# Banded attention and two feed-forward layers: six norms traced a part per step, and four conversion steps instead of five

## The chip, the cores and the metric

The kernel runs on one core of a Trainium2 chip. The core has five engines with a queue each that is worked off in order: TensorE (PE in the rows) for matmuls, VectorE (DVE), ScalarE (ACT), GpSimd (POOL) and SyncE (SP), which here only issues transfers (DMA). The metric is the device time of one execution in microseconds.

## The reference

Three stages follow each other, each on the result of the one before. The attention has 4 batches of 8 heads with 512 local and 32 global positions and a head width of 64. Local queries see the global keys and the local keys within 32 positions; global queries see all.

```python
    s_ll = np.where(mask, s_ll, -1000000000.0)
    s_l = np.concatenate([s_lg, s_ll], axis=-1)
    out_l = np.matmul(sm(s_l), np.concatenate([v_g, v_l], axis=2))
    ...
    rms = np.sqrt(np.mean(x * x, axis=-1, keepdims=True) + 1e-06)
    xn = x / rms * rms_g
    g = xn @ w_gate
    silu = g * (1.0 / (1.0 + np.exp(-g)))
    x = silu * (xn @ w_val) @ w_out
    ...
    h = x @ w_in
    g = P(h) / (Q(h) + 1e-06)
    return g @ w_out
```

The second stage (FFN1) has 2304 tokens, a width of 512 and a hidden width of 1536, the third (FFN2) a hidden width of 2048 and a rational function with P of third and Q of second degree. The weights arrive in 64-bit floating point.

## The kernel before

**Stages.** The loop over t from 0 to 35 (in the function that the program prints below) runs the attention, a pair of heads and half of the positions at a time: `att.step(t, between)` traces scores (`psS`), softmax (`p`, `pt`), products (`psO`, `on`) and the turned result (`psX`, copied to `x` at L420); `qt` at L338 are the turned queries of a step. For each pair of heads there is also a part for the global queries (`psG`, `pg`, `psGT`, `ptg`, `psOg`, `og`, `psGX`). Between these pieces `unit()` traces units of FFN1, 60 of them within the loop; FFN1 has three groups of weights by eight blocks of tokens, in the order 1, 0, 3, 2, 5, 4, 7, 6. A unit multiplies the split activations `xt` (L615, L616: a rounded part and its rest) by `w_g` and `w_v` (L625, L626, L629: `psg`, `psv`), applies the gate (L640 to L644: `a`, `ah`, `al`) and multiplies by `w_o` (L653 to L655: `psA`). After the loop comes the rest of FFN1, then FFN2.

**Norms.** Before the first unit of a block its tokens are normed. `norm_stages` is a generator with two `yield`s, so it has three parts: squares on ScalarE (L584, L585, L587, L589) and their sums on GpSimd (L586, L588, L590); then the sum over channels by a matmul `psN` (L593), L594 on VectorE and L595 on ScalarE; then L598 to L600 twice and the scaling L603 on VectorE. `norm_step()` runs the next part of the oldest norm. `split` runs whatever parts are left when a block's `xt` is made.

**Weights.** `Weights.stages` turns a 64-bit weight tile `raw` into two 32-bit ones, in four steps of a generator: L83 and L85 on ScalarE (L85 works in place on `raw`, so it needs the transfer of `raw` to have landed), L91, L92 and L95 on VectorE, L99 on VectorE, and L104 on ScalarE with the subtraction L105 on GpSimd. `wts.step` moves two such jobs on by one step and starts another when one is done. The transfers of `raw` (`raw_g`, `raw_v`, `raw_o`) are issued by SyncE at L66, in one queue with the loads of attention inputs at L216 (`vw`, `vn`, `gin`, `qin`, `kin`); a `vw` buffer is loaded, and then rounded off by small copies `vw<-vw`, once the `psO` that read it is done.

**What sets the order.** The code only traces instructions. A scheduler orders every engine's queue by priority, and by place in the trace at like priority. `att.step` is traced at an offset of 50 from t = 5, the norm parts at one of 200 (a higher one goes first), units and conversion steps at plain priority.

Of the kernel before, what the change touches and what calls it, by code (L numbers as in the profile page):

```python
# [788 lines left out]
def kernel(  # L789
# [20 lines left out]
    def load_consts():  # L810
        nc.sync.dma_start(out=gam, in_=rms_g.rearrange("(c p) -> p c", p=128))
        nc.sync.dma_start(out=av, in_=bass.AP(tensor=ca.tensor, offset=ca.offset, ap=[[0, 128], [1, 4]]))
        nc.sync.dma_start(out=bv, in_=bass.AP(tensor=cb.tensor, offset=cb.offset, ap=[[0, 128], [1, 2]]))
# [29 lines left out]
    def norm_step():  # L843
        if norms and next(norms[0], StopIteration) is StopIteration:
            norms.pop(0)

    def unit():
        done[0] += 1
        next(units, None)
# [24 lines left out]
    for t in range(LAST + 1):  # L874
        if t >= SECOND:
            target[0] = 6 + (IN_ATTN - 6) * (t + 1 - SECOND) / (LAST + 1 - SECOND)
        elif t >= START:
            target[0] = 6 * (t + 1 - START) / (SECOND - START)
        gate = [i.ins for i in (att.last_exp, att.last_ttr) if i]
        with tc.high_priority(offset=50) if t >= START else nullcontext():  # L880
            att.step(t, between)
        while done[0] < target[0] - 1:
            unit()
        if t == 2:
            load_consts()
        if t % 4 == 2 and t > 12:
            norms.append(ffn.norm(ORD[(t - 6) // 4]))
        elif t in (4, 8):
            norms.append(ffn.norm(ORD[t // 4 - 1]))
        with tc.high_priority(offset=200):  # L890
            for _ in range(3):
                norm_step()
        for _ in range(2 if t > 2 else 0):
            if loads:
                with tc.issue_after(att.last_dma.ins):
                    loads.pop(0)()
        with ExitStack() as late:
            for i in gate if t <= 8 else ():
                late.enter_context(tc.issue_after(i))
            for _ in range((0, 0, 0, 2, 5, 4, 4, 4)[t] if t < 8 else 2):  # L900
                wts.step(nc.gpsimd)
    while done[0] < IN_ATTN:
        unit()
# [94 lines left out]
```

## Time and profile before

| | us |
|---|---|
| median of 3 runs | 1048.28 (1047.91 to 1048.77) |
| profiled execution | 1043.17 |
| its span | 1041.4 |
| TensorE busy in it | 987.8 |
| VectorE busy | 779.1 |
| ScalarE busy | 633.0 |
| GpSimd busy | 189.2 |

The profile covers one execution; its span is the time from its first to its last instruction. All durations come from this one execution, whose time is 5.1 us under the median of the runs. Busy times of engines overlap. The granted clock of TensorE is a share of its full 2.4 GHz: at 0.50 it runs at 1.2 GHz.

### The profile page before, as it was taken

The page shows a single profiled execution, that of the slowest core. Times are in us where ns is not written, and L with a number is a line of the kernel's source. Part 1 is how long each engine was busy: PE and PEld are TensorE (multiplying, and loading weights), DVE is VectorE, ACT ScalarE, POOL GpSimd, SP SyncE. Part 2 cuts the span into 40 slices and gives each one's busy share as a digit, 9 for nine tenths or more (in the row PEclk, how much of TensorE's full clock was granted, in tenths as well). Part 3 has the DMA queues.
Part 4 walks back from the last instruction along what each step waited for, and adds up shares of the span by engine and source line. Part 5 has one row for each costly group of instructions (what it writes and reads, how often), then busy time and mean ns, then how long its engine had stood idle before and what let it go on. Part 6 is the DMA issues. An engine that isn't in the chain of part 4 may idle for free.

```text
span 1041.4 us, 23568 instructions
## 1 busy us (share of the span) xinstructions
PE 987.8 (95%) x9376; PEld 900.6 (86%) x9376; DVE 779.1 (75%) x1848; ACT 633.0 (61%) x1442; POOL 189.2 (18%) x220
## 2 busy tenths in 40 slices
PE   7578989999989999999999999999999999999997
PEld 5366877887879999999999999989899889899895
DVE  6586553655549899884896444898988989889897
ACT  4546554645457774553754323777777778777685
POOL 5333221202120000000000002321222222222222
PEclk8669999999999999999999999999999999999999
DMA  9733645353143421542501106200000000000000
GB/s 239 202 106 80 142 115 130 82 142 82 31 165 140 163 82 50 212 166 82 179 24 41 42 1 202 82 1 24 8 1 31 1 2 31 1 32 1 1 31 21
DMA packets 103311, 82.38 MB, mean 79 GB/s; under 512 B 63137, under 2 KB 90785, under 8 KB 103201
## 3 DMA queue, kind: packets, MB, share of 16 engines
q1 hardware_dynamic: 101472, 74.58, 24.2%
q0 software_dynamic: 1728, 6.29, 1.8%
q8 instruction: 74, 1.21, 0.5%
q14 instruction: 37, 0.30, 0.1%
HBM read 62.64 MB, written 10.75 MB: 70 GB/s over the span
## 4 chain that ended last, share of the span: by engine, by line
PE 80%; DVE 9%; DMA 5%; ACT 3%; SPq 1%; issue 1%; POOL 0%; ACTq 0%; POOLq 0%; DVEq 0%
PE psH L731 6%; PE psH L733 6%; PE psH L732 6%; PE psB L767 6%; PE psB L768 6%; PE psB L769 5%; PE psg L625 5%; PE psA L653 4%; PE psv L625 4%; PE psg L626 4%; PE psv L626 4%; PE psA L655 4%; PE psA L654 4%; PE psv L629 4%; PE psg L629 4%; PE psS L364 3%
## 5 line engine op out<-in xcount | busy, mean ns | idle before, releaser
L758 POOL TENSOR_TENSOR gl<-p,gh 128x384 fp32r<-128x384 f32 (+1 forms) x94 | 95.2, 1013 | 281.2 <-ACT gh L756 239.1
L731 PE MATMUL psH<-yt,w_h 128*128 128x384 f32 (+1 forms) x384 | 125.6, 328 | 0.5 <-DVE y L661 0.5
L732 PE MATMUL psH<-yt,w_h 128*128 128x384 f32 (+1 forms) x384 | 125.6, 327 | 0.0
L733 PE MATMUL psH<-yt,w_h 128*128 128x384 f32 (+1 forms) x384 | 123.5, 328 | 0.0
L625 PE MATMUL psg<-xt,w_g 128*128 128x288 f32 (+1 forms) x384 | 113.8, 299 | 7.7 <-ACT xt L615 7.6
L653 PE MATMUL psA<-ah,w_o 128*128 128x288 f32 (+1 forms) x384 | 112.8, 297 | 2.4 <-DVE y L661 1.1
L625 PE MATMUL psv<-xt,w_v 128*128 128x288 f32 (+1 forms) x384 | 111.1, 292 | 0.0
L626 PE MATMUL psv<-xt,w_v 128*128 128x288 f32 (+1 forms) x384 | 110.7, 290 | 0.0
L767 PE MATMUL psB<-w_p,gh 128*128 128x512 f32 x272 | 108.0, 397 | 2.9 <-ACT gh L756 2.9
L626 PE MATMUL psg<-xt,w_g 128*128 128x288 f32 (+1 forms) x384 | 110.3, 290 | 0.0
L654 PE MATMUL psA<-ah,w_o 128*128 128x288 f32 (+1 forms) x384 | 109.9, 290 | 0.0
L655 PE MATMUL psA<-al,w_o 128*128 128x288 f32 (+1 forms) x384 | 109.4, 290 | 0.0
L768 PE MATMUL psB<-w_p,gh 128*128 128x512 f32 x272 | 107.5, 395 | 0.0
L629 PE MATMUL psv<-xt,w_v 128*128 128x288 f32 (+1 forms) x384 | 103.4, 291 | 0.0
L629 PE MATMUL psg<-xt,w_g 128*128 128x288 f32 (+1 forms) x384 | 102.6, 289 | 0.0
L741 DVE SCALAR_TENSOR_TENSOR q<-q,bv,t 128x384 f32<-128x384 f32 (+1 forms) x96 | 67.6, 704 | 29.6 <-ACT q L739 29.4
L769 PE MATMUL psB<-w_p,gl 128*128 128x512 f32 x272 | 84.7, 395 | 0.0
L625 PEld LDWEIGHTS psg<-xt,w_g 128*128 128x128 f32 x384 | 72.7, 190 | 10.5 <-ACT xt L615 8.2
L751 ACT ACTIVATE r<-q,cq 128x384 f32<-128x384 f32 (+1 forms) x96 | 57.6, 600 | 36.7 <-DVE q L741 36.0
L653 PEld LDWEIGHTS psA<-ah,w_o 128*128 128x128 f32 x384 | 72.9, 190 | 4.4 <-DVE y L661 1.5
L731 PEld LDWEIGHTS psH<-yt,w_h 128*128 128x128 f32 x384 | 72.3, 188 | 3.9 <-DVE y L661 0.8
L732 PEld LDWEIGHTS psH<-yt,w_h 128*128 128x128 f32 x384 | 72.3, 188 | 3.7
(176 smaller groups left out, 2635.6 us busy)
## 6 DMA issues: line engine op xcount, KB each, us to landing
raw_h<-in_moe_w_in_dram SPq DMA_DIRECT2D x16, 512.0 KB, 3.7
raw_p<-in_moe_w_out_dram SPq DMA_DIRECT2D x16, 512.0 KB, 4.5
vw<-vw SPq DMA_DIRECT2D x56, 130.0 KB, 2.6
raw_g<-in_moe_w_gate_dram SPq DMA_DIRECT2D x12, 512.0 KB, 4.2
raw_v<-in_moe_w_val_dram SPq DMA_DIRECT2D x12, 512.0 KB, 5.2
raw_o<-in_moe_w_out_dram SPq DMA_DIRECT2D x12, 512.0 KB, 6.0
vw<-in_v_l_dram SPq DMA_DIRECT2D x62, 80.0 KB, 2.5
out_dram<-o SPq DMA_DIRECT2D x17, 256.0 KB, 2.0
```

The costliest lines, as they stand in the source:

```text
L625: nc.tensor.matmul(ps[j], part(j, 0, c), xt[c][:, 0], start=(c == 0), stop=False)
L626: nc.tensor.matmul(ps[j], part(j, 1, c), xt[c][:, 0], start=False, stop=False)
L629: nc.tensor.matmul(ps[j], part(j, 0, c), xt[c][:, 1], start=False, stop=(c == 3))
L653: nc.tensor.matmul(ps, wh, ah, start=(i == 0), stop=False)
L654: nc.tensor.matmul(ps, wl, ah, start=False, stop=False)
L655: nc.tensor.matmul(ps, wh, al, start=False, stop=(i == 3))
L731: nc.tensor.matmul(ph[:, :n], wh, yt[c][:, 0, :n], start=(c == 0), stop=False)
L732: nc.tensor.matmul(ph[:, :n], wl, yt[c][:, 0, :n], start=False, stop=False)
L733: nc.tensor.matmul(ph[:, :n], wh, yt[c][:, 1, :n], start=False, stop=(c == 3))
L767: nc.tensor.matmul(acc[m], gh[:, sl], wh, start=(k == 0), stop=False)
L768: nc.tensor.matmul(acc[m], gh[:, sl], wl, start=False, stop=False)
L769: nc.tensor.matmul(acc[m], gl[:, sl], wh, start=False, stop=(k == NC2 - 1))
```

## The change

```diff
--- before.py
+++ after.py
@@ -887,9 +887,12 @@
             norms.append(ffn.norm(ORD[(t - 6) // 4]))
         elif t in (4, 8):
             norms.append(ffn.norm(ORD[t // 4 - 1]))
-        with tc.high_priority(offset=200):
-            for _ in range(3):
-                norm_step()
+        if t < 14:
+            with tc.high_priority(offset=200):
+                for _ in range(3):
+                    norm_step()
+        else:
+            norm_step()
         for _ in range(2 if t > 2 else 0):
             if loads:
                 with tc.issue_after(att.last_dma.ins):
@@ -897,7 +900,7 @@
         with ExitStack() as late:
             for i in gate if t <= 8 else ():
                 late.enter_context(tc.issue_after(i))
-            for _ in range((0, 0, 0, 2, 5, 4, 4, 4)[t] if t < 8 else 2):
+            for _ in range((0, 0, 0, 2, 4, 4, 4, 4)[t] if t < 8 else 2):
                 wts.step(nc.gpsimd)
     while done[0] < IN_ATTN:
         unit()
```

Up to t = 13 the norms are traced as before: all three parts in the step in which a norm is made, at the raised priority. This covers blocks 1 (t = 4) and 0 (t = 8). From t = 14 a step runs one part, at plain priority. A norm is made every four steps (t = 14, 18, 22, 26, 30, 34 for blocks 3, 2, 5, 4, 7, 6), so its parts are traced at t, t + 1 and t + 2; the third part of block 6 falls behind the loop. The second edit takes one `wts.step` out of t = 4; as the queue of jobs stays the same, each later call does what the one before it did. No instruction is added or removed. Line numbers behind L890 rise by three.

In ScalarE's queue near 28 us of the trace, `raw_g_2` is the gate weight of the third tile of the first group and `qt4` the queries of step 4. Before:

```order
L85 ACTIVATE raw_v_1_205<-raw_v_1_205 128x512
L85 ACTIVATE raw_g_2_550<-raw_g_2_550 128x512
L584 ACTIVATE st0_1_694<-x0_0_70 128x256
L338 ACTIVATE qt4_564<-psQ4_563 128x256
L104 ACTIVATE w_g_0_726<-cv0_554 128x512
L104 ACTIVATE w_v_0_733<-cv1_560 128x512
```

In the changed kernel the copy L85 of `raw_g_2` has left this place; it stands 13 rows later, behind the exponentials L382 of step 4:

```order
L382 ACTIVATE p4_671<-p4_671,nm_108 128x128 x4
L104 ACTIVATE w_g_1_879<-cv2_730 128x512
L85 ACTIVATE raw_g_2_550<-raw_g_2_550 128x512
L85 ACTIVATE raw_v_2_552<-raw_v_2_552 128x512
L104 ACTIVATE w_v_1_886<-cv3_739 128x512
L420 ACTIVATE x0_1_71<-psX3_633 128x256
L440 ACTIVATE pg_107,gs_111<-psG0_0_682,gm_110 128x512
L441 ACTIVATE pg_107,gs_111<-psG0_1_683,gm_110 128x32
L85 ACTIVATE raw_g_3_718<-raw_g_3_718 128x512
L338 ACTIVATE qt5_747<-psQ5_746 128x256
```

In that piece the copy of the next tile, `raw_g_3`, also stands ahead of `qt5`. Before, at the same place of ScalarE's queue, it stood behind `qt5`:

```order
L440 ACTIVATE pg_107,gs_111<-psG0_0_682,gm_110 128x512
L441 ACTIVATE pg_107,gs_111<-psG0_1_683,gm_110 128x32
L589 ACTIVATE st1_1_695<-x0_1_71 128x256
L338 ACTIVATE qt5_754<-psQ5_753 128x256
L85 ACTIVATE raw_g_3_718<-raw_g_3_718 128x512
```

The copy L85 of `raw_g_2` has moved behind the work of step 4, and that of `raw_g_3` has moved ahead of `qt5`.

In VectorE's queue near 57 us (norm of block 1, `st_1`; `cv_903` is the conversion of the gate weight of `raw_g_3`, `dn` and `on` belong to the attention's fifth step, `og` to its global part; the numbers behind the names tell buffers apart), the piece of the difference:

```order
-L91 TENSOR_SCALAR cv_903<-cv_903 128x512
+L408 RECIPROCAL dn<-dn 128x4
 L600 SCALAR_TENSOR_TENSOR st_1_695<-st_1_696,st_1_695 128x256
-L408 RECIPROCAL dn<-dn 128x4
-L471 TENSOR_SCALAR og_1038<-psOg_1015,gs 128x128
-L92 TENSOR_SCALAR cv_903<-cv_903 128x512
+L410 TENSOR_TENSOR on_1004<-psO_981,dn 128x256
 L598 SCALAR_TENSOR_TENSOR st_1_696<-st_1_695,st_1_694 128x256
-L410 TENSOR_TENSOR on_1013<-psO_990,dn 128x256
-L95 SCALAR_TENSOR_TENSOR cv_903<-raw_g_718,cv_903 128x512
+L471 TENSOR_SCALAR og_1029<-psOg_1006,gs 128x128
```

The three operations of `cv_903` have left this stretch for one behind L603, and `og` (L471) stands behind the first L600 and the second L598 instead of between the first L600 and `cv_903`.

In TensorE's queue at the end of the attention (steps 29 to 31, norm of block 6), before:

```order
L459 MATMUL psOg7_4705<-vn0_104,ptg7_4563 32x64 x2
L478 MATMUL psGX7_4730<-ident_112,og7_4728 128x128
L387 MATMUL psT31_4734<-ident_112,p31_4657 128x128 x4
L416 MATMUL psX29_4796<-ident_112,on29_4699 128x128 x2
L397 MATMUL psO31_4846<-vw3_103,pt31_4739 32x65 x16
L416 MATMUL psX30_4867<-ident_112,on30_4794 128x128 x2
L416 MATMUL psX31_4905<-ident_112,on31_4865 128x128 x2
L593 MATMUL psN6_4919<-st0_6_4909,ones_214 128x288
L653 MATMUL psA0_5_0_4933<-ah5_0_4232,w_o_0_1237 128x256
```

The changed kernel's rows up to the same matmul `psN6`:

```order
L625 MATMUL psv_4_1_4934<-xt0_4_3_4835,w_v_1_886 128x288
L626 MATMUL psv_4_1_4934<-xt0_4_3_4835,w_v_1_886 128x288
L629 MATMUL psg_4_1_4933<-xt0_4_2_4832,w_g_1_879 128x288
L629 MATMUL psv_4_1_4934<-xt0_4_2_4832,w_v_1_886 128x288
L629 MATMUL psg_4_1_4933<-xt0_4_3_4835,w_g_1_879 128x288
L629 MATMUL psv_4_1_4934<-xt0_4_3_4835,w_v_1_886 128x288
L416 MATMUL psX31_4905<-ident_112,on31_4865 128x128 x2
L593 MATMUL psN6_4947<-st0_6_4909,ones_214 128x288
L653 MATMUL psA0_5_1_5022<-ah5_0_4222,w_o_0_1237 128x256
```

The matmuls of `psGX7` to `psX30` have moved apart and ahead, among those of units 0 and 1 of block 4; `psX31` and `psN6` follow the last of unit 1, and `psA0_5_0` stands ahead of them (not shown), so that `psA0_5_1` comes straight behind `psN6`.

## Rows read from the trace of the kernel before

**Rows 1.** Page, part 1: engine, busy us, share, instructions.
```profile
PE 987.8 (95%) x9376; PEld 900.6 (86%) x9376; DVE 779.1 (75%) x1848; ACT 633.0 (61%) x1442; POOL 189.2 (18%) x220
```

**Rows 2.** Table of stretches: TensorE and other engines' busy us, then granted clock.
```profile
26.00:52.00 26.00, 13.09 (x170) 8.29 (x167) 14.51 (x40) 14.61 (x37) 8.19 (x7) 0.63 0.75 202
52.00:78.00 26.00, 20.35 (x306) 15.64 (x304) 21.87 (x58) 13.00 (x30) 9.88 (x10) 0.69 0.35 107
...
286.00:312.00 26.00, 21.57 (x231) 19.16 (x232) 12.28 (x33) 13.45 (x30) 6.67 (x9) 0.93 0.47 158
312.00:900.00 588.00, 585.83 (x3917) 560.89 (x3916) 474.00 (x939) 364.50 (x774) 70.44 (x74) 1.00 0.20 70
```

**Rows 3.** Timeline, ScalarE: start, duration, instruction, idle before and its releaser.
```profile
27.56 0.68 ACT L85 ACTIVATE raw_v<-raw_v 128x512 int32<-128x512 uint32 x1
36.71 0.65 ACT L85 ACTIVATE raw_g<-raw_g 128x512 int32<-128x512 uint32 x1 [8.47 <-DMA raw_g<-in_moe_w_gate_dram]
...
37.58 0.36 ACT L338 ACTIVATE qt<-psQ 128x256 f32<-128x256 f32 x1
...
49.97 0.39 ACT L338 ACTIVATE qt<-psQ 128x256 f32<-128x256 f32 x1
```

**Rows 4.** Timeline, TensorE, 26 to 63 us.
```profile
37.99 0.69 PE L416 MATMUL psX<-ident,on 128*128 128x128 f32 x2 [9.15 <-ACT qt L338]
...
47.77 0.66 PE L416 MATMUL psX<-ident,on 128*128 128x128 f32 x2 [3.63 <-DVE on L410]
...
62.32 0.58 PE L625 MATMUL psg<-xt,w_g 128*128 128x256 f32 x1 [5.16 <-ACT xt L615]
```

**Rows 5.** Timeline, SyncE's DMA issues, 30 to 50 us.
```profile
32.81 0.45 SPq L66 DMA_DIRECT2D raw_g<-in_moe_w_gate_dram  x1
...
36.16 5.38 SPq L216 DMA_DIRECT2D vw<-in_v_l_dram  x4
...
42.65 1.25 SPq L216 DMA_DIRECT2D vw<-vw  x2
43.94 0.59 SPq L66 DMA_DIRECT2D raw_g<-in_moe_w_gate_dram  x1
```

**Rows 6.** Timeline, VectorE, 48 to 66 us.
```profile
53.52 1.64 DVE L95 SCALAR_TENSOR_TENSOR cv<-raw_v,cv 128x512 int32<-128x512 int32 x1
...
57.09 1.48 DVE L600 SCALAR_TENSOR_TENSOR st<-st,st 128x256 f32<-128x256 f32 x1
...
59.82 0.68 DVE L95 SCALAR_TENSOR_TENSOR cv<-raw_g,cv 128x512 int32<-128x512 int32 x1
...
60.87 0.42 DVE L600 SCALAR_TENSOR_TENSOR st<-st,st 128x256 f32<-128x256 f32 x1
61.33 2.15 DVE L603 SCALAR_TENSOR_TENSOR x<-x,gam,st 128x256 f32<-128x256 f32 x4
```

**Rows 7.** Timeline, GpSimd, 40 to 64 us.
```profile
53.11 1.50 POOL L105 TENSOR_TENSOR w_g<-cv,w_g 128x512 fp32r<-128x512 f32 x1 [1.71 <-ACT w_g L104]
56.84 1.45 POOL L105 TENSOR_TENSOR w_v<-cv,w_v 128x512 fp32r<-128x512 f32 x1 [2.23 <-ACT w_v L104]
```

**Rows 8.** Timeline, TensorE, 150 to 157 us.
```profile
153.49 0.58 PE L625 MATMUL psg<-xt,w_g 128*128 128x256 f32 x1 [1.94 <-ACT xt L615]
...
155.36 0.44 PE L653 MATMUL psA<-ah,w_o 128*128 128x288 f32 x1
```

**Rows 9.** TensorE's waits, 160 to 286 us: waiter, releaser, us, times, longest.
```profile
PE psQ L325 <- ACT x L420: 3.0, 6, 0.6
```

**Rows 10.** Timeline, TensorE, 290 to 310 us.
```profile
295.19 0.33 PE L478 MATMUL psGX<-ident,og 128*128 128x128 f32 x1 [0.60 <-DVE og L471]
...
298.35 0.41 PE L416 MATMUL psX<-ident,on 128*128 128x128 f32 x2 [0.68 <-DVE on L410]
300.70 1.33 PE L593 MATMUL psN<-st,ones 128*128 128x288 f32 x2 [1.94 <-POOL st L590]
...
305.10 0.38 PE L653 MATMUL psA<-ah,w_o 128*128 128x256 f32 x1 [0.93 <-ACT y L659]
```

## Prediction

> **What bounds the kernel now.** I read the page's first rows, then a table of stretches, then the waits and single instructions of those stretches where TensorE stands. TensorE is busy 987.8 us of the span [rows 1], so at most some 54 us could be had at all. The table tells where: from 312 to 900 us TensorE is busy 585.83 of 588 us at full clock, while from 26 to 52 it is busy only 13.09 of 26 us at a granted clock of 0.63, from 52 to 78 20.35 us at 0.69, and from 286 to 312, where the attention ends, 21.57 us at 0.93 [rows 2]. The change can pay only in the stretches with holes; 312 to 900 just moves with what comes before.
>
> The largest hole is at the start. TensorE stands 9.15 us before 37.99 us, put down to ScalarE's `qt` (L338) [rows 4]. On ScalarE the hole is one instruction ahead: the in-place copy L85 of `raw_g_2` stands 8.47 us for its transfer, from some 28.2 to 36.71 us, and the `qt` behind it, whose input was long there, starts at 37.58 [rows 3]. So a weight conversion that nobody needs yet holds up the attention. Two more holes follow, 3.63 us before 47.77 (for VectorE's `on`) and 5.16 us before 62.32, where the first FFN unit waits for the split `xt` of block 1 [rows 4]. At the end of the attention stand 0.60, 0.68, 1.94 and 0.93 us before 295.19, 298.35, 300.70 and 305.10 [rows 10].
>
> **The change part by part.** *Fewer conversion steps at t = 4.* No instruction is added or removed; four `wts.step` calls stand where five stood, the rest come one call later. What this moves is seen in ScalarE's order: the copy L85 of `raw_g_2` goes from ahead of `qt4` to behind the exponentials of step 4, 13 rows later. Without it ScalarE goes on at 28.2 us, `qt4` starts near 28.6 instead of 37.58, and all behind it starts 9.0 us earlier, until the next thing that does not depend on it. That next thing is also in the order: L85 of `raw_g_3` now stands ahead of `qt5`, where it stood behind. Before, its transfer was issued at 43.94 us [rows 5]; the one of `raw_g_2` took 36.71 - 32.81 = 3.9 us from issue to use [rows 3, 5]. The issue at 43.94 was late because SyncE stood in the four `vw` loads from 36.16, 5.38 us, the buffers of which TensorE's `psO` had to release. With TensorE 9 us earlier I let them go at the rate of an issue, 0.45 to 0.59 us each [rows 5]: done by 38.2 us, the two `gin` loads by 39.2. The two `vw` copies behind read what the `vw` loads brought, so I give these 2 us to land: start near 40.2, done in 1.25 us [rows 5], so `raw_g_3` is issued at 41.5 and there at 45.4 to 45.7. ScalarE, 9.0 us ahead of its former time there, is ready for it near 41.2 and stands some 4.4 us; the 8.47 us become 4.4, and `qt5` starts near 46.2 instead of 49.97 [rows 3], **3.8 us earlier**.
>
> From `qt5` to the first FFN unit the chain is `pt4`, the norm of block 1 (matmul, L594, L595, L598 to L600 twice, L603) and `xt`: 62.32 - 49.97 = 12.35 us before. On VectorE three operations of the conversion `cv6` leave it, the longest of which, L95, took 0.68 us at 59.82 [rows 6]; I put the three at 1.3 us, twice that. I count 0.5 of it, since the `og` (L471) that now stands among the last norm steps waits for TensorE's `psOg`, which comes 3.8 us earlier and no more. So the first unit starts **4.3 us earlier**, near 58.0. The bounds: 1.5 us if the issue of `raw_g_3` stays at 43.94 (there at 47.8, `qt5` at 48.5); 5.8 if all of the 1.3 us counts and VectorE's long operations below become short.
>
> VectorE shows L95 once with 1.64 and once with 0.68 us, and L600 with 1.48 and 0.42 us; the long ones are at 53.52 and 57.09, and GpSimd runs its subtraction L105 from 53.11 for 1.50 and from 56.84 for 1.45 us, beside both [rows 6, 7]. These two are 2.0 us longer than their twins. The Trainium skill (GPSIMD Engine Reference, section 8, Key points) says that GpSimd shares its memory interfaces with VectorE, with contention for VectorE instructions with two inputs in SBUF; the trace agrees with 1.64 against 0.68 us. By that rule the gain hangs on where L105 falls now: if it falls beside L603 or L600 as before, the first unit gains 4.3 us; if beside nothing, up to 5.8 us. I take the first.
>
> What hides the conversions that come later? None of TensorE's holes has a conversion as its releaser [rows 4, 10], and the conversions move forward with ScalarE anyway: I cost their lateness at nothing. Without that cover the price would be a wait of TensorE for a weight, at most the 1.3 us by which one more conversion step keeps VectorE, which is inside the bounds. After 62 us TensorE is nearly dense and its loads follow its own progress, so I let the shift persist to the end.
>
> *Norms at plain priority, a part a step.* The same instructions; the squares of a block are traced at t, the matmul at t + 1, the scaling at t + 2, and the scheduler places them among the rest. For block 3 the order of VectorE, ScalarE and GpSimd shows no change that matters, and the stall of 1.94 us before 153.49 [rows 8] stays. For blocks 2, 5, 4 and 7 the norm slides some tens of rows back on each engine, and the fine order of units and attention changes with it. Between 160 and 286 us TensorE's named waits are small: 3.0 us in six for an `x` copy of ScalarE [rows 9]. In the new order other matmuls (a second product, `psO`) stand ahead of some of these; I take **0.6 us**, a fifth of it, with 1.7 us (over half) as the upper bound and a loss of 2.9 us as the lower one: one stall as that of block 3, 1.94 us, and behind it a lower clock. The eight matmuls from 153.49 to 155.36 took 1.87 us there [rows 8], half of it, an estimate of 0.9 us, more than at double clock.
>
> At the end the order changes most. Before, `psGX7`, `psT31`, `psX29`, `psO31`, `psX30`, `psX31` and `psN6` follow each other with no FFN matmul between, and three of the four waits of [rows 10] lie among them; the fourth, 0.93 us, is that of `psA0_5_1` for the sum of `psA0_5_0` just ahead. Now `psA0_5_0` and the last 12 matmuls of unit `psg_4_1` lie among them, some 1.4 us each by the 0.12 us a matmul of the estimate above, and `psX31` and `psN6` come last. Of the waits 0.60, 0.68 and 0.93 us find work ahead of them, **2.2 us**; the 1.94 us of `psN6` for GpSimd's sum of squares stays, since still nothing stands between `psX31` and it. Bounds: 1.2 us if a wait reappears at `psX31`, 3.6 us if the lower clock of this stretch (0.93 [rows 2], 26 us) goes: 7% of the 21.6 us busy is 1.5 us.
>
> **The sum.** 4.3 + 0.6 + 2.2 = 7.1 us. The profiled execution took 1043.17 us (span 1041.4), 5.1 under the median of 1048.28; as I know no reason why that difference should change, the profiled one should come to 1036.1 and the median to **1041.2**. From the bounds: gains of 1.5 - 2.9 + 1.2 = -0.2 to 5.8 + 1.7 + 3.6 = 11.1 us, so 1037.2 to 1048.5; both ends need all three at once.
>
> **The rivals.** (1) *The wait only moves.* `raw_g_3` is issued no earlier, or the matmuls that the new order puts into the holes wait themselves. For it: SyncE's queue is in order and stood 5.38 us at one buffer. Against: what it stood for comes 9 us earlier. Early gain 1.5, the rest 0.6 + 2.2: 4.3 us, **1044.0**. (2) *No measurable change.* VectorE takes back the early gain between 60 and 80 us, where the conversion steps now fall, and the end gains 1.2 us: 1048.28 - 1.5 = **1046.8**. For it: VectorE is busy 21.87 of the 26 us from 52 to 78 [rows 2]. Against: TensorE was not seen to wait for a weight. (3) *Slower.* A norm at plain priority, spread over three steps, comes too late for its first unit; TensorE then waits as before 153.49, at 1.94 + 0.9 = 2.9 us each. Five blocks (2, 5, 4, 7, 6) can. It decides from 7.1 / 2.9 = 2.5, so from three blocks; with four it is 1048.28 - 7.1 + 11.6 = **1052.8**. For it: block 3 had no time to spare even at raised priority. Against: block 3 is not later in the new order, and the later blocks are four steps apart. (4) *More.* TensorE's clock. Granted 0.63 from 26 to 52, when TensorE had been idle for 9.15 us, and 0.69 from 52 to 78 behind the other holes [rows 2, 4]; at the full clock a part of the matmuls on the chain from 48 to 57 us would halve. If it returns for half of these 9 us, 2.3 us more: 9.4 us, **1038.9**. The Trainium skill (TensorE: Matmul & The Clock Gate, Part 1) says that the clock falls to half after idling and returns after sustained work; by that rule this needs dense work ahead of 48 us. I see a hole of some 4 us still there.
>
> **How the numbers follow.** Forecast 0.44 (1039.5 to 1043), rival 1 0.20, rival 2 0.14, rival 3 0.10, rival 4 0.12. The range 1036.8 to 1047.6 leaves out rival 3, a quarter of 2 and a third of 4, under 0.2. A measurement tells 0.2%, 2.1 us, from no change. Faster by more: 0.44 + 0.20 + 0.12 = 0.76; within: most of rival 2, 0.14; slower: rival 3, 0.10.
>
> **What would show it.** In the profile after: ScalarE's 8.47 us gone, a wait of 3 to 5 us at L85 `raw_g` near 41 to 46 us, the first `psg` of the FFN near 58 instead of 62.32, no wait of over 0.3 us between 285 and 297 us but one near 2 us ahead of the last L593, and 1.94 us still ahead of block 3's first unit. Wrong would make it: a `psg` that waits for `xt` more than once after 100 us; a first `psg` later than 60.5; or VectorE as the releaser of new waits from 60 to 110 us.

## The result, and the profile after

| | before | after |
|---|---|---|
| median of 4 runs each, us | 1048.53 (1047.91 to 1050.17) | 1063.22 (1059.88 to 1065.33) |
| ratio | | 1.0138, 95% interval 1.0115 to 1.0162 |
| profiled execution, us | 1043.17 | 1063.15 |
| its span, us | 1041.4 | 1061.4 |
| TensorE busy, us | 987.8 | 1007.7 |
| span less TensorE's busy time, us | 53.6 | 53.7 |

The changed kernel is slower by 1.4%, some 14.7 us, where 7.1 us less was forecast. The profiled executions lie 20.0 us apart, since the one of before was 5 us under its median; runs of the kernel before were between 1043.6 and 1052.9 us in the experiments, so differences of a few us between two profiles are not explained below. One execution among those of the experiments, of the kernel with the scores of step 31 together, took 3245 us and is left out of its ratio.

The first rows of the page after, against [rows 1], hold the finding already. TensorE has the same 9376 records, stands idle as long as before (53.7 against 53.6 us), and is busy 19.9 us longer (x counts records: a score or a product has two, a step's 16 products 32, a matmul of the FFN has one):

```profile
span 1061.4 us, 23576 instructions
...
PE 1007.7 (95%) x9376; PEld 909.5 (86%) x9376; DVE 780.1 (74%) x1848; ACT 633.2 (60%) x1442; POOL 190.4 (18%) x220
```

So no wait can hold the loss: it lies in the time that counts as busy. The table of stretches (after the stretch and its length: busy us of TensorE, weight loads, VectorE, ScalarE, GpSimd, each with its count; then granted clock, DMA share, GB/s) shows one place at once. From 286 to 312 us TensorE is busy all of the 26 us, with only 174 records at a clock of 0.74, where before it did 231 in 21.57 us at 0.93 [rows 2]:

```profile
26.00:52.00 26.00, 11.59 (x153) 7.01 (x147) 13.12 (x39) 13.35 (x32) 7.72 (x7) 0.70 0.84 213
52.00:78.00 26.00, 18.87 (x332) 15.32 (x331) 21.93 (x63) 15.04 (x36) 10.88 (x10) 0.82 0.36 107
...
286.00:312.00 26.00, 26.00 (x174) 19.15 (x175) 8.00 (x28) 6.33 (x19) 4.77 (x7) 0.74 0.00 1
```

How the steps of the attention stand against the kernel before (start of the first matmul, after less before): the first FFN unit, 62.32 us before [rows 4], starts 3.0 us earlier; the scores of step 8 are 0.2 us late, of step 12 2.9, of step 18 6.0, of step 27 9.1, of step 31 9.5; the last scores of step 31 end 20.7 us late, and FFN2 starts 20.0 us late. The early gain came, was gone by 93 us, and the loss grew in many small steps and one large one.

The scores `psS` and products `psO` carry it. Grouped by line from 78 to 345 us (count | busy us, mean ns | idle before and its releasers), before:

```profile
L364 PE MATMUL psS<-kt,qt 64*32 64x96 f32 x800 | 28.0, 253 | 0.5 <-ACT qt L338 0.3
L364 PE MATMUL psS<-kgt,qt 64*32 64x32 f32 x800 | 24.0, 191 | 0.0
L397 PE MATMUL psO<-vw,pt 128*32 128x65 f32 x834 | 22.3, 223 | 0.4 <-PE psS L364 0.3
```

and after:

```profile
L364 PE MATMUL psS<-kt,qt 64*32 64x96 f32 x800 | 34.2, 260 | 0.3
...
L397 PE MATMUL psO<-vw,pt 128*32 128x65 f32 x832 | 30.8, 228 | 0.4 <-PE psS L364 0.2 <-ACT pt L389 0.2
...
L364 PE MATMUL psS<-kgt,qt 64*32 64x32 f32 x800 | 28.1, 195 | 0.0
```

The same scores and products (some 2432 records) cost 74.3 us before and 93.1 after, 18.8 more. Their mean length hardly moves (253 to 260, 223 to 228 ns); what moves is how closely they follow each other. A piece of the timeline before has the 32 records of a step's `psO` started within 0.6 us, the next matmul at 297.23:

```profile
296.64 0.66 PE L397 MATMUL psO<-vw,pt 128*32 128x65 f32 x32
297.23 0.44 PE L416 MATMUL psX<-ident,on 128*128 128x128 f32 x2
```

After, the scores of step 31 and the products of step 30 alternate one by one (two records each), from 292.6 to 302.9 us, in rows like these:

```profile
293.12 0.30 PE L397 MATMUL psO<-vw,pt 128*32 128x65 f32 x2
293.36 0.24 PE L364 MATMUL psS<-kgt,qt 64*32 64x32 f32 x2
293.53 0.38 PE L397 MATMUL psO<-vw,pt 128*32 128x65 f32 x2
...
296.06 0.31 PE L364 MATMUL psS<-kgt,qt 64*32 64x32 f32 x2
296.30 0.43 PE L397 MATMUL psO<-vw,pt 128*32 128x65 f32 x2
296.65 0.31 PE L364 MATMUL psS<-kgt,qt 64*32 64x32 f32 x2
296.90 0.43 PE L397 MATMUL psO<-vw,pt 128*32 128x65 f32 x2
297.25 0.52 PE L364 MATMUL psS<-kt,qt 64*32 64x96 f32 x2
```

From 296 us on, one of `psS` and one of `psO` take 0.59 to 0.81 us together. The turn of a product and a score with `kgt` took 0.41 us at 293.12, at the clock's full level, and takes 0.60 at 296.30, at 0.50. TensorE is never idle there by the record, and starts few matmuls.

### The profile page after: what moved, and what is told of

It is laid out like the page before. It is cut to its first block, busy times and chain, and to the rows that moved or that the text cites. A ratio compares the mean times of both kernels' runs of the same rounds, so it can differ in the third digit from the quotient of the medians.

```text
span 1061.4 us, 23576 instructions
## 1 busy us (share of the span) xinstructions
PE 1007.7 (95%) x9376; PEld 909.5 (86%) x9376; DVE 780.1 (74%) x1848; ACT 633.2 (60%) x1442; POOL 190.4 (18%) x220
## 4 chain that ended last, share of the span: by engine, by line
PE 83%; DVE 8%; DMA 5%; ACT 2%; SPq 1%; issue 1%; POOL 0%; ACTq 0%; DVEq 0%; POOLq 0%
PE psH L731 6%; PE psH L733 6%; PE psH L732 6%; PE psB L767 5%; PE psB L768 5%; PE psB L769 5%; PE psg L625 5%; PE psA L653 4%; PE psg L629 4%; PE psv L626 4%; PE psv L625 4%; PE psg L626 4%; PE psA L654 4%; PE psA L655 4%; PE psv L629 4%; PE psS L364 4%
## 5 line engine op out<-in xcount | busy, mean ns | idle before, releaser
L625 PE MATMUL psg<-xt,w_g 128*128 128x288 f32 (+1 forms) x384 | 114.9, 302 | 9.1 <-ACT xt L615 8.6
L626 PE MATMUL psg<-xt,w_g 128*128 128x288 f32 (+1 forms) x384 | 111.2, 292 | 0.0
L629 PE MATMUL psg<-xt,w_g 128*128 128x288 f32 (+1 forms) x384 | 104.6, 294 | 0.0
```

Of the source, the lines that this page charges most:

```text
L625: nc.tensor.matmul(ps[j], part(j, 0, c), xt[c][:, 0], start=(c == 0), stop=False)
L626: nc.tensor.matmul(ps[j], part(j, 1, c), xt[c][:, 0], start=False, stop=False)
L629: nc.tensor.matmul(ps[j], part(j, 0, c), xt[c][:, 1], start=False, stop=(c == 3))
```

## The experiments

**A count to test by.** In TensorE's order I count the changes of kind: places where a matmul follows one of another kind. The kinds go by the rows and columns of TensorE's array that a matmul uses, as the rows above give them: scores (64 by 32), products (128 by 32), global scores (128 by 64), global products (128 by 32, kept apart from products), small transposes, and full 128 by 128 ones. Before has 267, the changed kernel 346. The theory (A): each costs a fixed time.

**Each edit alone.** The conversion edit alone (`(0, 0, 0, 2, 4, 4, 4, 4)`, norms as before):

> Only the conversion edit (four steps at t = 4), norms as before. Theory A: the loss lies in TensorE's order, where matmuls of different kinds (scores, products, global products, full 128 by 128 ones) alternate; before has 267 changes of kind in its order, the changed kernel 346, and 23 us lost between 59 and 340 us over 79 changes is 0.29 us a change. This kernel has 269: it keeps the early 3 us and pays 0.6, so 1046 us, faster than before. Theory B: the early shift itself spoils the later part (loads and conversions fall elsewhere): slower than before, 1055 to 1063 us.

Measured: 1050.89 us against 1047.34, ratio 1.0028 (1.0004 to 1.0053). It is a little slower, not faster: theory A, with 1046, missed it by 5 us, and theory B, with 1055 or more, by 4; this is taken up below. The norm edit alone (the `if t < 14` and its `else`, five conversion steps):

> Only the norm edit, five conversion steps at t = 4 as before. Theory A: 342 changes of kind against 267, 75 more at 0.29 us: before + 21.8 = 1070 us, no early gain. Theory B: the norm edit alone costs little: within 3 us of before.

Measured: 1064.81 us, 1.0174 (1.0143 to 1.0205). The norm edit is the one that costs; theory A gave 1070, 5 us too much. TensorE is busy 1003.1 of 1059.6 us there.

**What of the norm edit.** Both edits, but three parts at plain priority in one step, and a part a step at the raised priority:

```diff
         else:
-            norm_step()
+            for _ in range(3):
+                norm_step()
```

> Both edits, but the three parts of a norm all in the step where it is made, at plain priority. 293 changes of kind. Theory A: -3 + 26 x 0.29 = +4.5, 1053 us. Theory C (the loss is plain priority: norms come late and units wait for xt): as slow as the changed kernel, near 1063 us, with waits for xt of TensorE above 5 us in all after 78 us.

```diff
         else:
-            norm_step()
+            with tc.high_priority(offset=200):
+                norm_step()
```

> Both edits, a part of a norm a step, but at the raised priority of 200. 305 changes of kind. Theory A: -3 + 38 x 0.29 = +8, 1056.5 us. Theory C: with the priority back no loss is left: 1045 us. Theory D (the loss is the spreading over three steps, whatever the priority): near 1063 us.

Measured: 1052.70 us, 1.0070 (1.0040 to 1.0101), and 1057.00 us, 1.0105 (1.0079 to 1.0131). Theory A had 1053 and 1056.5. The plain priority alone costs a part, the spreading alone costs a part: either moves the order of the matmuls, and the time goes with the changes of kind. Theory C, which put the loss down to the plain priority, and theory D, to the spreading, are both out as the one cause. Waits for `xt` are not it: in the changed kernel they are 2.6 us in two after 78 us (waiter, releaser, us, times, longest), with 1.9 us in one before [rows 8]:

```profile
PE psg L625 <- ACT xt L615: 2.6, 2, 2.0
```

**One place undone.** The changed kernel, with the scores of step 31 alone at a higher priority, so that they stand together; TensorE's order is the same up to them:

```diff
+        with self.tc.high_priority(offset=1000) if s == 31 else nullcontext():
             for c in range(2):
                 for j in range(4):
```

> The changed kernel with one thing more: the score matmuls of step 31 alone are traced at a raised priority of 1000, so that they stand together in TensorE's order instead of in pairs among FFN matmuls and products; the order is the same up to that step. 317 changes of kind instead of 346. Theory A (changes of kind cost): psS31, which took 17.0 us from first to last in the changed kernel and 5.8 before, becomes short, 8 to 11 us come back: 1052 to 1055 us. Rival (the stretch is slow for another reason, the clock falls there or a transfer is awaited): same as the changed kernel, 1063 us.

Measured: 1051.73 us, 1.0047 (1.0029 to 1.0066): 9.5 us of the loss are gone by the ratios (0.0091 of 1047), from an edit of one step's order. The stretch after the first scores of step 31, in the changed kernel and in this one:

```profile
288.00:304.00 16.00, 16.00 (x106) 9.33 (x105) 4.68 (x19) 0.78 (x3) 0.00 (x0) 0.68 0.00 1
```

```profile
286.00:304.00 18.00, 18.00 (x198) 16.39 (x193) 9.59 (x31) 7.83 (x22) 6.05 (x8) 1.00 0.01 2
```

106 records in 16 us at a clock of 0.68 against 198 in 18 us at 1.00. So of the large step a part is the alternation and a part is that the clock falls under it. An estimate of the clock's part in the turns: those from 293.6 to 302.9 us stand at 0.50, and with 0.60 us instead of 0.41 a turn that is some 3 us.

**All places undone.** Scores at 3000 and products at 1000 from step 8 on, so that the scores of a step run as one piece and its products as another ("pieces together" from here on), in the changed kernel and in the kernel before:

```diff
 def scores(self, s):
+        with self.tc.high_priority(offset=3000) if s >= 8 else nullcontext():
             for c in range(2):
 def pv(self, s):
+        with self.tc.high_priority(offset=1000) if s >= 8 else nullcontext():
             for c in range(2):
```

> The changed kernel with the scores of all steps from 8 on at a priority raised by 3000 and their products by 1000, so that each runs as one piece. 206 changes of kind instead of 346. Theory A at 0.24 us each: 34 us less than the changed kernel, 1030 us; with some new holes where FFN matmuls no longer fill in, up to 1042. Rival (alternation is what hides the waits of the attention, changes are cheap): gain under 5 us, 1058 us or more, with more idle time of TensorE.

> The kernel before with the same raised priorities for scores and products from step 8 on, nothing else. 209 changes of kind instead of 267. Theory A: 58 x 0.24 = 14 us less than before, 1034 us; with new holes 1034 to 1042. Rival: no gain, 1047 us or more.

Measured: 1029.33 us, 0.9828 (0.9806 to 0.9851), and 1035.33 us, 0.9890 (0.9864 to 0.9916); theory A had 1030 and 1034. The pages, of the changed kernel with pieces together and of the kernel before with them:

```profile
span 1028.0 us, 23570 instructions
...
PE 975.0 (95%) x9376; PEld 894.4 (87%) x9376; DVE 778.5 (76%) x1848; ACT 632.8 (62%) x1442; POOL 189.2 (18%) x220
```

```profile
span 1036.2 us, 23570 instructions
...
PE 980.0 (95%) x9376; PEld 899.3 (87%) x9376; DVE 777.9 (75%) x1848; ACT 633.4 (61%) x1442; POOL 189.7 (18%) x220
```

Against the changed kernel TensorE is busy 32.7 us less (975.0 for 1007.7) and idle as long (53.0 for 53.7 us). The scores and products of 78 to 345 us cost 66.0 us instead of 93.1, which is 27.1 of the 32.7; in the kernel before with pieces together they cost 66.1. The alternation had hidden nothing.

**The price alone.** Only the matmuls, without a wait between them:

> No attention and no FFN: only the matmuls in question, on loaded data, without any wait between them, twice over: 64 scores in a piece, 64 products in a piece, then 32 times two scores and two products in turn, 32 times one full matmul (128 by 128 by 256) and two scores in turn, 32 times one full matmul and two products in turn, with 80 full matmuls ahead of each. Theory A: in a piece 64 scores take near 1 us and 64 products near 1.3 us, while the turns take 0.3 to 0.6 us each, 10 to 19 us for 32, some 0.15 to 0.25 us a change of kind, more at the lower clock. Rival (changes of kind are free, the loss in the kernel is waits): the turns take no more than the sum of the pieces, 2.3 us for scores and products.

The timeline shows the turns of two scores and two products from 41.15 us on (two records each), and the first full matmul behind the 32nd turn:

```profile
41.15 0.36 PE L75 MATMUL psS<-kt,qt 64*32 64x96 f32 x4
41.44 0.31 PE L80 MATMUL psO<-vw,pt 128*32 128x65 f32 x4
41.67 0.25 PE L75 MATMUL psS<-kg,qt 64*32 64x32 f32 x4
41.85 0.31 PE L80 MATMUL psO<-vw,pt 128*32 128x65 f32 x4
```

```profile
56.23 0.98 PE L84 MATMUL psF<-xt,w 128*128 128x256 f32 x6
```

In a piece, the 64 scores start at 120.36 and the next full matmul at 122.09; the 64 products run from 131.87 to 133.82:

```profile
120.36 0.38 PE L75 MATMUL psS<-kt,qt 64*32 64x96 f32 x12
```

```profile
122.09 0.74 PE L84 MATMUL psF<-xt,w 128*128 128x256 f32 x4
```

```profile
131.87 2.02 PE L80 MATMUL psO<-vw,pt 128*32 128x65 f32 x128
133.82 0.86 PE L84 MATMUL psF<-xt,w 128*128 128x256 f32 x5
```

So 32 turns take 56.23 - 41.15 = 15.08 us, and the same matmuls in two pieces 1.73 + 1.95 = 3.68 (longer than the 1 and 1.3 us expected): 11.40 us more over 64 changes, **0.18 us a change**. With 80 full matmuls taking 131.87 - 122.09 = 9.78 us, the turns of a full matmul with two scores (66.13 to 83.34, 17.21 us) and with two products (93.24 to 110.58, 17.34 us) give 0.18 us a change as well. The clock was granted in full, in the turns as in the piece of full matmuls:

```profile
41.10:56.20 15.10, 15.10 (x258) 9.12 (x256) 0.00 (x0) 0.00 (x0) 1.00 0.01 2
...
122.20:131.80 9.60, 9.60 (x80) 9.54 (x80) 0.00 (x0) 0.00 (x0) 1.00 0.01 2
```

**The count against the time.** Ratios with changes of kind, sorted:

| kernel | changes | ratio | TensorE busy / idle in its profile, us |
|---|---|---|---|
| changed, together from step 4 | 184 | 0.9766 | 973.7 / 49.9 |
| before + conversion edit, together | 205 | 0.9926 | 979.8 / 60.6 |
| changed, together from step 8 | 206 | 0.9828 | 975.0 / 53.0 |
| before, together | 209 | 0.9890 | 980.0 / 56.2 |
| before + norm edit, together | 210 | 0.9869 | 976.3 / 55.2 |
| before | 267 | 1 | 987.8 / 53.6 |
| conversion edit alone | 269 | 1.0028 | 988.8 / 63.0 |
| changed, norm in one step | 293 | 1.0070 | 991.3 / 59.6 |
| changed, norm at 200 | 305 | 1.0105 | 1001.2 / 52.6 |
| changed, step 31 together | 317 | 1.0047 | 994.8 / 54.3 |
| norm edit alone | 342 | 1.0174 | 1003.1 / 56.5 |
| changed | 346 | 1.0138 | 1007.7 / 53.7 |

Four kernels stand in the table both as they are and with pieces together from step 8, which differ in the order alone. Over the ratios this is 32.5 us for 140 changes in the changed kernel, 31.9 for 132 with the norm edit alone, 11.5 for 58 in the kernel before and 10.7 for 64 with the conversion edit alone: 0.17 to 0.24 us a change, and the 0.18 of the bare matmuls is most of it. Between kernels with different edits the count does not settle everything: at 205 to 210 changes the times spread over 10 us. The two with the conversion edit alone are slow for their count; they are idle 60.6 and 63.0 us, more than most. The changed kernel with pieces together, which differs in nothing but the order, is the best measured here; begun at step 4 instead of 8 it has 184 changes:

> The changed kernel with scores and products kept together from step 4 on instead of 8 (1029.3 us with 206 changes): 184 changes. At 0.18 to 0.24 us a change 4 to 5 us less, 1024.5 us. Rival: the early steps wait for ScalarE and VectorE, a change of kind there costs nothing since TensorE stands anyway, 1029 us.

Measured: 1023.13 us, 0.9766 (0.9744 to 0.9788), 6.5 us better than from step 8 by the ratios.

**What the two edits are worth without the alternation.** With all four cases at 205 to 210 changes:

> As the run with the kernel before and its scores and products kept together (1035.3 us, 209 changes of kind), with the conversion edit alone added (205 changes). What is left of the forecast without the alternation: the conversion edit was to bring 4.3 us, of which 3.0 showed at the first FFN unit: 1031 to 1032.5 us. Rival (VectorE takes the early gain back between 70 and 95 us, as in the run with the conversion edit alone): 1035 us.

> As the kernel before with scores and products kept together (1035.3 us, 209 changes), with the norm edit alone added (210 changes). By the forecast the norm edit brings 0.6 + 2.2 = 2.8 us: 1032.5 us. Rival (its small gains do not add up, or the norms come late): 1035 us or more.

Measured: 1040.53 us, 0.9926 (0.9906 to 0.9945), and 1034.07 us, 0.9869 (0.9842 to 0.9895). The norm edit alone brings some 2 us of the forecast 2.8, less than the intervals tell apart. The conversion edit alone costs 3.8 us (in the first pair, without the pieces together, 2.9), where 1031 to 1032.5 us was expected and 1035 by the rival; with the norm edit it brings 4.3 us (0.9869 to 0.9828). Both figures are at the edge of the intervals. Both edits together bring 6.5 us (0.9890 to 0.9828), against 7.1 forecast. The two are not additive, and the profile of the conversion edit alone shows one place where. At the end of the attention the copy `y` (L659) that `psA0_5_1` needs stands on ScalarE behind L83 and L85 of a second weight, `raw_v`, for whose transfer ScalarE waits 1.63 us; before, `y` stood ahead of that L83. TensorE waits 3.40 us for it, where it was 0.93 before [rows 10]:

```profile
308.24 0.66 ACT L83 ACTIVATE cv<-raw_v 128x512 f32<-128x512 f32 x1 [1.63 <-DMA raw_v<-in_moe_w_val_dram]
308.81 0.66 ACT L85 ACTIVATE raw_v<-raw_v 128x512 int32<-128x512 uint32 x1
309.36 0.37 ACT L659 ACTIVATE y<-psA 128x256 f32<-128x256 f32 x1
```

```profile
309.79 0.58 PE L653 MATMUL psA<-ah,w_o 128*128 128x256 f32 x1 [3.40 <-ACT y L659]
```

In the changed kernel this wait is 0.64 us, for VectorE (below). With pieces together the wait for `y` is there again, 3.78 us with the conversion edit and 1.8 without it, and one of 2.7 us for an `xt` between 345 and 450 us comes with the edit; these two, some 4.7 us, are about the 4.4 us by which its idle time is the longer (60.6 for 56.2). Why that `xt` comes late was not followed up, nor were the other waits of the conversion edit alone (6.0 us from 330 to 680 us, 2.1 before); its profile was also 2.7 us above the median of its kernel.

## Why the prediction was wrong

**The step that failed** is the one on the norms in the middle: "In the new order other matmuls (a second product, `psO`) stand ahead of some of these; I take 0.6 us". It treated a new fine order of TensorE's matmuls as filling for waits, free in itself, with a loss of 2.9 us at most. The waits that it priced did shrink, from 3.0 us in six [rows 9] to 2.1 us in four; what it put at nothing was the busy time. The order of the changed kernel has 79 more changes of kind than that of before. At the 0.18 us measured, they are 14 us; with some 3 us for the clock that fell under the densest of them, 17 of the 18.8 us by which scores and products grew are accounted for. The Trainium skill (TensorEngine Tiling (Array Packing), Key Properties) says that changing the tiling mode drains TensorE; the page gives no time. The runs agree as far as they go, with 0.18 us a change; what happens within one they do not show. The forecast should have weighed this rule, since both orders were open to it: of the 79 changes 37 are between scores and full matmuls and 31 between scores and products, and they can be read in the order without any trace.

**The waits, term by term.** The early gain was of the right kind and too large. ScalarE's 8.47 us before `raw_g_2` [rows 3] are gone, `qt4` is at 27.96, and the new wait is where it was put, at L85 of `raw_g_3`, with 6.17 us instead of 4.4 (ScalarE, after):

```profile
27.96 0.36 ACT L338 ACTIVATE qt<-psQ 128x256 f32<-128x256 f32 x1
...
47.42 0.67 ACT L85 ACTIVATE raw_g<-raw_g 128x512 int32<-128x512 uint32 x1 [6.17 <-DMA raw_g<-in_moe_w_gate_dram]
47.98 0.37 ACT L338 ACTIVATE qt<-psQ 128x256 f32<-128x256 f32 x1
```

The term that was off is SyncE's. The four `vw` loads went out by 38.63 us as forecast (38.2), but the `vw` copies behind them started at 42.11 instead of 40.2, so that `raw_g_3` was issued at 43.38, not 41.5, little ahead of before's 43.94 [rows 5]:

```profile
36.50 2.13 SPq L216 DMA_DIRECT2D vw<-in_v_l_dram  x4
...
42.11 1.23 SPq L216 DMA_DIRECT2D vw<-vw  x2
43.38 0.59 SPq L66 DMA_DIRECT2D raw_g<-in_moe_w_gate_dram  x1
```

`qt5` gained 2.0 us (47.98 for 49.97) instead of 3.8. That is rival 1 for this term, which had 1.5. From `qt5` to the first FFN unit it is 11.3 us instead of 12.35, 1.0 us less where 0.5 was counted. Of VectorE's two long operations one is left: GpSimd's L105, from 53.61 us for 1.74, stands beside the first L598 now, whose twin takes 0.41 us, and L600 takes 0.42:

```profile
54.15 1.48 DVE L598 SCALAR_TENSOR_TENSOR st<-st,st 128x256 f32<-128x256 f32 x1
...
56.12 0.42 DVE L600 SCALAR_TENSOR_TENSOR st<-st,st 128x256 f32<-128x256 f32 x1
```

The first FFN unit then started at 59.29, 3.0 us earlier and not 4.3:

```profile
37.70 0.66 PE L416 MATMUL psX<-ident,on 128*128 128x128 f32 x2 [5.14 <-DVE on L410]
...
48.40 0.92 PE L452 MATMUL psGT<-ident,pg 128*128 128x128 f32 x3 [6.93 <-ACT qt L338]
...
59.29 0.58 PE L625 MATMUL psg<-xt,w_g 128*128 128x256 f32 x1 [4.62 <-ACT xt L615]
```

By step 8 this gain is gone in the changed kernel, and down to 1.2 us with pieces together, though up to there the pieces are not yet raised. Rival 2 (VectorE takes it back) had the outcome right, but the cause only in small part: from 59 us on TensorE waits 1.9 us for VectorE's `ptg`, 1.1 before, and the clock of the changed kernel is 0.82 and 0.75 from 76 to 80 and 80 to 84 us, where before it is 1.00.

The end went nearly as forecast: of 0.60, 0.68 and 0.93 us [rows 10], 2.2 us that were all to go, 0.64 us is left, a gain of 1.6; the wait of `psN6` stays, 2.23 us for 1.94:

```profile
320.56 1.01 PE L593 MATMUL psN<-st,ones 128*128 128x288 f32 x2 [2.23 <-POOL st L590]
322.21 0.55 PE L653 MATMUL psA<-ah,w_o 128*128 128x256 f32 x1 [0.64 <-DVE st L594]
```

The stall ahead of block 3's first unit stayed, 1.99 us. Rival 3 had the right direction for a wrong reason: norms that come late. Its sign came, a second wait for `xt` after 100 us, of 0.60 us; but two waits of 2.6 us in all are not five of 2.9.

The lateness of the conversions, put at nothing, was safe only with both edits: with the conversion edit alone TensorE waits for a `y` behind them, as shown above.

Three figures of the prediction do not come out of its own terms. The upper bound of the early gain adds to 3.8 + 1.3 + 2.0 = 7.1 us, not 5.8; the range 1036.8 to 1047.6 is not the one that its bounds give, 1037.2 to 1048.5; and rival 2 takes off 1.5 us where its text gains 1.2. The measured 1063.22 us lies outside all of these.

**The sum in hindsight.** With the pieces together in both kernels, the change brings 6.5 us. That this is near the 7.1 forecast is partly luck: 4.3 us were to come from the conversion edit and 2.8 from the norm edit, and alone they bring -3.8 and some 2; and of the 8.2 us between the two profiles only 3.2 are idle time, the kind that the forecast counted, and 5.0 busy time. Against it stands the order: 79 changes at 0.18 to 0.23 us, 14 to 18 us, and in step 31 a clock that fell. From 14.7 us slower, as the change is, to 6.5 us faster, with pieces together on both sides, it is 21 us. The forecast had no term for this.

## What to carry to other kernels

Where a kernel mixes small matmuls that use part of the array with full ones, count in TensorE's order how often the kind changes, before and after an edit; here a change costs 0.18 us at the full clock, without idle time, without a wait, and inside "busy". When TensorE's busy time grows at the same number of matmuls, read the timeline for pairs in turn, and group by line: same count, same mean, more busy. And an edit that adds no instruction can still reorder much: the norm edit alone brought 75 changes of kind. Keep small matmuls of one step together: a raised priority around them from step 8 on was worth 1.1% on the kernel before, and with it the changed kernel ends 1.7% under before (2.3% from step 4 on) instead of 1.4% over.

## What was not expected of the hardware

That TensorE's clock falls under work that the record shows as unbroken: 0.50, the lower of its two levels, from 296 to 304 us of the changed kernel, while scores and products alternate one by one and TensorE is busy all the time by the record (26 records in the first 4 us of it). Before it fell, near 293.6 us, scores had alternated so with full matmuls from 287.8 us on, and with products from 292.6:

```profile
296.00:300.00 4.00, 4.00 (x26) 2.16 (x24) 0.00 (x0) 0.00 (x0) 0.00 (x0) 0.50 0.00 0
300.00:304.00 4.00, 4.00 (x23) 2.56 (x22) 1.61 (x11) 0.39 (x2) 0.00 (x0) 0.50 0.00 0
```

In the bare turns, 15 us long, the clock stayed at 1.00; but those are turns of two and two matmuls, and here it is one and one. Whether that makes the difference was not tried and stays open. The price of a change at the full clock is the same, 0.18 us, between scores and products, scores and full matmuls, products and full matmuls.
